# Attention from the seventh tile on in pairs of tiles, 52 weight tiles converted without a maximum, and a new table of attention's release times

## The chip, the core and the metric

One core of a Trainium2 chip runs the whole program. The metric is the device time of one execution in microseconds (us), lower is better. TensorE (PE) does the matmuls, VectorE (DVE), ScalarE (ACT) and GpSimd (POOL) the elementwise work, SyncE (SP) issues the DMAs.

## What is computed

The reference, cut to its core: chunked attention, then two feed-forward layers over all 4608 tokens. The weights come as 64-bit floats.

```python
# q, k, v: (8, 8, 576, 64); chunks of 64 tokens
scores = scale * np.matmul(q_c, k_c.transpose(0, 1, 2, 4, 3))
scores = scores - np.max(scores, axis=-1, keepdims=True)
attn = np.exp(scores)
attn = attn / (np.sum(attn, axis=-1, keepdims=True) + 1e-09)
out = np.matmul(attn, v_c)
...
x = out.transpose(0, 2, 1, 3).reshape(4608, 512)
h = np.maximum(x @ w_in, 0.0)            # w_in (512, 2048)
x = h * h @ w_out                        # w_out (2048, 512)
gate = 1.0 / (1.0 + np.exp(-(x @ w_gate)))   # (512, 1536)
return gate * (x @ w_val) @ w_out2       # (1536, 512)
```

## The kernel before, in words

Attention works on 36 tiles of 128 tokens, all eight heads of a tile together. Six tiles fill two raw buffers of 384 tokens (`raw1`), from which the first feed-forward layer takes its operands. That layer (`plain_unit` for the first six tiles, then `Unit` in the form of Strassen's scheme with seven products) works on these 768 tokens while TensorE does the attention of the next six tiles in between. Every product is a sum over three float32r matmuls per operand pair (high times high, low times high, high times low), so TensorE's work comes in groups of three matmuls with 384 columns (line L689). The operands are made by `split`: ACT writes the high part (L479), DVE the low part (L484). The raw buffers are subtracted from each other on POOL (L493).

For one tile, `attention` has these steps: k and q are turned round on TensorE (L858; from tile 12 on q by DVE from another load), 32 small 64x64 matmuls make the scores in two PSUM banks (L878), DVE takes maximum and difference for each bank (L904, L906), ACT the exponential (L909), DVE the sum (L910) and its inverse (L913, L914), POOL or, from tile 12 on, DVE multiplies (L493), TensorE turns the result round (L924), 32 small matmuls mix it with v (L940), and ACT puts the two banks into `raw1` (L958).

`to_float32` makes a float32 tile from 128x512 words of 64 bits: ACT takes the upper word's absolute value as a float (L526) and scales the lower word (L530), DVE bounds the first from below (L533), shifts it (L537) and puts the sign in (L544), POOL adds the lower word (L551). It is called with `raws`, fixed buffers, for the 16 tiles of the first layer's output weights and the 36 of the second layer (52 tiles), and without for the 16 tiles of the first layer's input weights.

The order on every engine is made by `Plan.run`, a list scheduler over jobs with costs in us. TensorE's jobs are of two kinds. Those of the stream "main", the products, keep their order. Those of the stream "att" are released by a table, `TIMES`: for each tile the due time of the steps k, q, S (scores), T (turning the result) and X (mixing), on an axis whose zero is the first product. At each free moment the ready job with the earliest due time is taken. `Plan.fill` puts matmuls of the identity (L1462) into gaps near the start.

```python
    for j in sorted(cands, key=lambda j: (j.due - self.STAY * (small and j.shared), j.n)):
        if not j.left and take(j):
```

## Time and profile before

| | us |
|---|---|
| median of 3 runs (1600.95 to 1603.32) | 1601.09 |
| profiled execution, its own time | 1601.8 |
| its span, first to last instruction | 1600.0 |
| PE busy in the span | 1584.4 |
| DVE busy | 1306.6 |
| ACT busy | 972.0 |
| POOL busy | 530.8 |

Busy times come from one profiled execution. A matmul's end is modelled, so neighbouring matmuls overlap in the profile; the distance between starts is what a matmul takes in a row of them. What lies outside the span is 1.8 us. A wait of TensorE shows as idle time, or as a start that comes later than the row before it would allow.

### The profile page before, as it was taken

What the parts mean: (1) busy time and instruction counts of PE and PEld (TensorE: products, weight loads), DVE (VectorE), ACT (ScalarE), POOL (GpSimd) and SP (SyncE); (2) the same over time, 40 slices, a digit from 0 to 9 for tenths busy, and PEclk for the clock granted to TensorE, in tenths of its full rate; (3) what the DMA queues carried; (4) which work ended last, traced back from release to release, by engine and by line L of the source; (5) the groups of instructions that cost most, each with busy time, mean ns of one, the idle gap of its engine ahead of it and who ended that gap; (6) DMA issues with size and microseconds to landing.
All of it is one profiled execution on the core that took longest, in us unless ns stands there. A gap on an engine that the chain in (4) does not pass through costs nothing.

```text
span 1600.0 us, 29686 instructions
## 1 busy us (share of the span) xinstructions
PE 1584.4 (99%) x10209; PEld 1387.7 (87%) x10209; DVE 1306.6 (82%) x2170; ACT 972.0 (61%) x1922; POOL 530.8 (33%) x432
## 2 busy tenths in 40 slices
PE   8999999999999999999999999999999999999999
PEld 6998999999998888899888898888888888888888
DVE  6968878797989998999998797743786748889886
ACT  7986676676876656566665665543565545555554
POOL 2452402021442111111266685643576641000000
PEclk9999999999999999999999999999999999999999
DMA  9965667677884848487787547586447577866562
GB/s 214 275 166 143 155 190 187 175 207 218 267 290 148 276 152 261 155 280 241 255 279 267 183 146 244 186 281 217 168 162 245 196 260 257 250 196 164 150 174 52
DMA packets 381991, 333.27 MB, mean 208 GB/s; under 512 B 231824, under 2 KB 292240, under 8 KB 381840
## 3 DMA queue, kind: packets, MB, share of 16 engines
q1 hardware_dynamic: 381840, 331.38, 67.8%
q8 instruction: 80, 1.31, 0.4%
q14 instruction: 71, 0.58, 0.1%
HBM read 209.13 MB, written 122.16 MB: 207 GB/s over the span
## 4 chain that ended last, share of the span: by engine, by line
PE 92%; DVE 3%; ACT 2%; DMA 1%; SPq 1%; issue 1%; POOL 0%; DVEq 0%; ACTq 0%
PE bank L689 51%; PE bank L1097 37%; SPq L457 1%; PE bank L878 1%; PE bank L940 1%; PE bank L924 1%; PE bank L858 1%; DMA wraw__750<-in_moe_w_in_dram 0%; DMA wf<-wf__3185 0%; PE bank L1077 0%; DMA k__326<-in_k_dram 0%; DVE T__2019 L484 0%; DMA gd<-b__3834 0%; DVE B__760 L484 0%; DMA ql__4671<-in_q_dram 0%
## 5 line engine op out<-in xcount | busy, mean ns | idle before, releaser
L551 POOL TENSOR_TENSOR wf__6958<-wf__6958,wr__6912 128x512 int32<-128x512 int32 x18 | 28.2, 1568 | 163.1 <-DVE wf__6958 L544 119.8
L551 POOL TENSOR_TENSOR wf__3185<-wf__3185,wr__3118 128x512 int32<-128x512 int32 x16 | 21.8, 1361 | 174.0 <-DVE wf__3185 L544 120.1
L551 POOL TENSOR_TENSOR wf__7071<-wf__7071,wr__6912 128x512 int32<-128x512 int32 x18 | 25.4, 1413 | 99.0 <-DVE wf__7071 L544 73.2
L493 POOL TENSOR_TENSOR raw__523<-raw__724,raw__523 128x384 f32<-128x384 f32 x20 | 24.2, 1229 | 30.1 <-DVE B__653 L484 12.3
L530 ACT ACTIVATE wr__6912<-wr__6912 128x512 int32<-128x512 uint32 x36 | 23.9, 665 | 0.0
L484 DVE TENSOR_TENSOR wx__7016<-ws__7143,wx__7016 128x512 fp32r<-128x512 f32 x18 | 17.8, 988 | 6.0 <-ACT wx__7016 L479 6.0
L493 POOL TENSOR_TENSOR ws__7143<-wf__7071 128x256 f32<-128x256 f32 x12 | 12.5, 1038 | 30.5 <-DVE wx__7684 L484 29.9
L484 DVE TENSOR_TENSOR wx__7684<-ws__7143,wx__7684 128x512 fp32r<-128x512 f32 x18 | 17.9, 997 | 4.7 <-ACT wx__7684 L479 4.7
L484 DVE TENSOR_TENSOR wx__7154<-wf__7071,wx__7154 128x256 fp32r<-128x256 f32 x18 | 14.2, 787 | 3.5 <-ACT wx__7154 L479 3.5
L479 ACT ACTIVATE wx__7154<-wf__7071 128x256 fp32r<-128x256 f32 x18 | 7.4, 411 | 15.8 <-POOL wf__7071 L551 15.6
L493 POOL TENSOR_TENSOR ws__7143<-ws__7143,wf__6958 128x256 f32<-128x256 f32 x18 | 16.2, 898 | 1.2
L533 DVE TENSOR_SCALAR wf__7071<-wf__7071 128x512 f32<-128x512 f32 x18 | 11.8, 653 | 5.6 <-ACT wf__7071 L526 5.4
L533 DVE TENSOR_SCALAR wf__6958<-wf__6958 128x512 f32<-128x512 f32 x18 | 10.3, 572 | 6.3 <-ACT wf__6958 L526 6.3
L493 POOL TENSOR_TENSOR ws__7143<-wf__6958,wf__7071 128x256 f32<-128x256 f32 x18 | 15.3, 848 | 0.3
L526 ACT ACTIVATE wf__3185<-wr__3118 128x512 f32<-128x512 f32 x16 | 10.6, 664 | 6.9 <-DMA wf<-wf__3185 6.9
L904 DVE TENSOR_REDUCE mx__379<-bank 128x4 f32<-128x256 f32 x16 | 6.6, 415 | 10.0 <-PE bank L878 10.0
L526 ACT ACTIVATE wf__7071<-wr__6912 128x512 f32<-128x512 f32 x18 | 11.9, 662 | 4.4 <-DMA wr__6912<-in_moe_w_gate_dram 1.9
L544 DVE SCALAR_TENSOR_TENSOR wf__6958<-wr__6912,wf__6958 128x512 int32<-128x512 int32 x18 | 14.1, 781 | 0.2
L533 DVE TENSOR_SCALAR wf__3185<-wf__3185 128x512 f32<-128x512 f32 x16 | 8.1, 506 | 7.5 <-ACT wf__3185 L526 7.5
L544 DVE SCALAR_TENSOR_TENSOR wf__7071<-wr__6912,wf__7071 128x512 int32<-128x512 int32 x18 | 13.8, 766 | 0.3
L526 ACT ACTIVATE wf__6958<-wr__6912 128x512 f32<-128x512 f32 x18 | 11.9, 659 | 3.1 <-DVE wod__6685 L484 1.5
L904 DVE TENSOR_REDUCE mx__2010<-bank 128x4 f32<-128x256 f32 x16 | 6.7, 417 | 8.5 <-PE bank L878 8.5
(5753 smaller groups left out, 6044.5 us busy)
## 6 DMA issues: line engine op xcount, KB each, us to landing
ad<-wx__7016 SPq DMA_DIRECT2D x27, 512.0 KB, 4.1
ad<-wx__7684 SPq DMA_DIRECT2D x27, 512.0 KB, 5.1
wr__3118<-in_moe_w_out_dram SPq DMA_DIRECT2D x16, 512.0 KB, 4.6
wr__6912<-in_moe_w_gate_dram SPq DMA_DIRECT2D x12, 512.0 KB, 4.7
wr__6912<-in_moe_w_val_dram SPq DMA_DIRECT2D x12, 512.0 KB, 4.4
wr__6912<-in_moe_w_out_dram SPq DMA_DIRECT2D x12, 512.0 KB, 3.9
ad<-wx__7154 SPq DMA_DIRECT2D x18, 256.0 KB, 3.7
wf<-wf__3185 SPq DMA_DIRECT2D x16, 256.0 KB, 4.5
```

Of the source, the lines that this page charges most:

```text
L457: nc.sync.dma_start(out=a, in_=b)
L484: lambda: nc.vector.tensor_tensor(out=lo(), in0=at(src, n, F32, off), in1=hi().bitcast(F32), op=ALU.subtract),
L493: eng, cost(eng, n), lambda: e.tensor_tensor(out=o(), in0=a(), in1=b(), op=op),
L526: nc.scalar.activation(out=at(w), in_=t[:, :, 1].bitcast(F32), func=ACTF.Abs)
L530: nc.scalar.activation(out=low, in_=low.bitcast(U32), func=ACTF.Copy, scale=2.0**-29)
L533: nc.vector.tensor_scalar_max(at(w), at(w), TINY)
L544: nc.vector.scalar_tensor_tensor(out=wi, in0=words()[:, :, 1], scalar=-0x40000000, in1=wi, op0=ALU.bitwise_and, op1=ALU.bitwise_or,)
L551: nc.gpsimd.tensor_tensor(out=wi, in0=wi, in1=words()[:, :, 0], op=ALU.add)
L689: nc.tensor.matmul(out=o, lhsT=at(op, P, F32R, wi * size + half * HB + kk * P), rhs=at(xb, n, F32R, xi * xsize + off), start=(first and kk ...
L858: nc.tensor.transpose(out=at(ps, P, F32, hp * P), in_=at(r, P, F32, hp * P), identity=ident)
L878: nc.tensor.matmul(out=o[c][to, hp, :], lhsT=qv[part, hp, tok], rhs=kv[part, hp, tok], start=True, stop=True,)
L1097: nc.tensor.matmul(out=at(ps[m], n), lhsT=at(w, P, F32R, wi * size + half * HB + m * P), rhs=at(x, n, F32R, xi * n), start=(first and kp = ...
```

## The change

From tile 6 on, `attention` takes two tiles at a time. The scores of both go into the same two banks (the second tile's into the second half), DVE and ACT work on 512 instead of 256 columns of a bank and on 1024 instead of 512 columns of the rest, one job mixes both tiles, and ACT's copies into `raw1` move both tiles at once where they lie in the same buffer (in every third pair they don't). Turning round stays one job for each tile. `TIMES` has a row for each of the 21 groups and other numbers throughout, also for the first six tiles, which stay single. In `to_float32` the 52 tiles with `raws` lose DVE's maximum; ACT scales by 2^-112 there, and shift counts and sign mask follow.

```diff
+        scale_, left, right, sign = (2.0**-112, 4, 1, -0x80000000) if raws else (1.0, 5, 2, -0x40000000)
...
-            nc.scalar.activation(out=at(w), in_=t[:, :, 1].bitcast(F32), func=ACTF.Abs)
+            nc.scalar.activation(out=at(w), in_=t[:, :, 1].bitcast(F32), func=ACTF.Abs, scale=scale_)
...
-                out=wi, in0=wi, scalar1=5, scalar2=2,
+                out=wi, in0=wi, scalar1=left, scalar2=right,
...
-        job("DVE", 0.41, bound, [w], [w], shared=True)
+        if not raws:
+            job("DVE", 0.41, bound, [w], [w], shared=True)
...
-        (-40, -40, -38, -34, -32),
...
-        (2.5, -1.25, -0.25, -2, 11.5),
...
+        ((-46.25,), (-46.25,), -47.25, (-40.25,), -38.25),
...
+        ((0.5, 4.25), (7.25, -1.5), 2.0, (-2.25, 8.75), 17.5),
...
+    FIRST = 6
+    GROUPS = [(t,) for t in range(FIRST)] + [(t, t + 1) for t in range(FIRST, NTL, 2)]
...
+        def chunk(c):
+            return at(ps_s[c], n * HB).rearrange("p (h k) -> p h k", k=CH)
...
-        job("PE", 0.53, scores, [qT, kT], ps_s, stream="att", at=nominal("S"), shared=True)
+        job("PE", 0.53 * n, scores, list(turned.values()), ps_s, stream="att", at=nominal("S"), shared=True)
...
-            job("DVE", 0.34, lambda c=c: nc.vector.tensor_reduce(
+            job("DVE", (0.34, 0.61)[n - 1], lambda c=c: nc.vector.tensor_reduce(
+                out=largest(c), in_=chunk(c), axis=AX.X, op=ALU.max), [ps_s[c]], [mx])
...
-        job("ACT", 0.53, lambda: nc.scalar.activation(out=at(a), in_=at(a), func=ACTF.Exp, scale=scale), [a], [a])
+        job("ACT", (0.53, 1.0)[n - 1], lambda: nc.scalar.activation(out=at(a), in_=at(a), func=ACTF.Exp, scale=scale),
+            [a], [a])
...
-        mixed = job("PE", 0.66, mix, [aT, vr], ps_x, stream="att", at=nominal("X"), shared=True)
+        mixed = job("PE", 0.66 * n, mix, [*turned_a, *values], ps_x, stream="att", at=nominal("X"), shared=True)
...
+        together = len(set(map(id, to))) == 1
         for c in range(2):
-            job("ACT", 0.27, lambda c=c: put(c), [ps_x[c]], [raw])
+            if together:
+                job("ACT", (0.27, 0.5)[n - 1], lambda c=c: put(c, 0, n), [ps_x[c]], [to[0]])
+                continue
+            for i in range(n):
+                job("ACT", 0.27, lambda c=c, i=i: put(c, i, 1), [ps_x[c]], [to[i]])
```

In the changed kernel the lines are three to twenty-five numbers away: products L692, k and q L855, scores L875, maximum and difference L900 and L902, exponential L905, sum L907, turning L924, mixing L944, puts L965.

How the order moves is seen best behind the first products on TensorE. In the kernel before, the scores of the first two tiles of the second group (each 32 matmuls, in rows of two) stand four product groups apart:

```order
L878 MATMUL bank_75<-kT_32768__876,qT_18432__801 64x64 x2
L878 MATMUL bank_73<-kT_32768__876,qT_18432__801 64x64 x2
L689 MATMUL bank_79<-T_3072_195584__818,wia_83968__799 128x384 x3
L689 MATMUL bank_79<-T_3072_192512__829,wia_83968__799 128x384 x3
L689 MATMUL bank_79<-B_3072_177152__856,wia_83968__799 128x384 x3
L689 MATMUL bank_79<-B_3072_174080__858,wia_83968__799 128x384 x3
L878 MATMUL bank_76<-kT_4608__808,qT_2560__607 64x64 x2
L878 MATMUL bank_77<-kT_4608__808,qT_2560__607 64x64 x2
```

In the changed kernel the same two tiles' scores stand in one block, later among the products, and in the same two banks:

```order
L875 MATMUL bank_75<-kT_28672__870,qT_14336__471 64x64 x2
L875 MATMUL bank_74<-kT_28672__870,qT_14336__471 64x64 x2
L875 MATMUL bank_75<-kT_8192__894,qT_12288__868 64x64 x2
L875 MATMUL bank_74<-kT_8192__894,qT_12288__868 64x64 x2
L875 MATMUL bank_75<-kT_8192__894,qT_12288__868 64x64 x2
L875 MATMUL bank_74<-kT_8192__894,qT_12288__868 64x64 x2
L875 MATMUL bank_75<-kT_8192__894,qT_12288__868 64x64 x2
L875 MATMUL bank_74<-kT_8192__894,qT_12288__868 64x64 x2
L855 MATMUL bank_77<-ident,k_10240__816 128x128 x4
L692 MATMUL bank_78<-B_3072_177152__826,wit_157696__818 128x384 x3
L692 MATMUL bank_78<-B_3072_174080__835,wit_157696__818 128x384 x3
```

What moved: two blocks with products between them became one. Over the whole program, behind the first product, TensorE's order goes from large matmuls to a block of small ones 37 times before and 26 times now, for the same 60 blocks (30 tiles, scores and mixing); behind the first product it has 33 fours of k and q turns before and 35 now, and 30 fours of the result in both.

On DVE, at the same place, before (`a` is the tile of scores, `wia` and `wit` are weight operands, `w` a weight tile in conversion):

```order
L904 TENSOR_REDUCE mx_0__379<-bank_75 128x4
L906 TENSOR_TENSOR a_18432__921<-bank_75,mx_0__379 128x4x64
L904 TENSOR_REDUCE mx_0__379<-bank_73 128x4
L906 TENSOR_TENSOR a_18432__921<-bank_73,mx_0__379 128x4x64
L484 TENSOR_TENSOR wia_79872__883<-w_8704__810,wia_79872__883 128x512
L533 TENSOR_SCALAR w_32768__929<-w_32768__929 128x512
```

and in the changed kernel:

```order
L484 TENSOR_TENSOR wia_79872__876<-w_18432__796,wia_79872__876 128x512
L535 TENSOR_SCALAR w_38912__910<-w_38912__910 128x512
L539 TENSOR_SCALAR w_38912__910<-w_38912__910 128x512
L900 TENSOR_REDUCE mx_5632__959<-bank_75 128x8
L902 TENSOR_TENSOR a_10240__968<-bank_75,mx_5632__959 128x8x64
L900 TENSOR_REDUCE mx_5632__959<-bank_74 128x8
L902 TENSOR_TENSOR a_10240__968<-bank_74,mx_5632__959 128x8x64
L484 TENSOR_TENSOR wit_149504__946<-w_0__846,wit_149504__946 128x512
```

What moved: four operations serve two tiles, each on twice the columns, and they now stand between the second weight group's first operand (`wia`) and its second (`wit`), where before they stood ahead of both. SP's first 18 loads (k, q and v of six tiles) and the first two weight loads behind them are the same in number in both programs.

## Rows read from the trace of the kernel before

**Rows 1.** The page: the span, and each engine's busy time, share and instructions.

```profile
span 1600.0 us, 29686 instructions
...
PE 1584.4 (99%) x10209; PEld 1387.7 (87%) x10209; DVE 1306.6 (82%) x2170; ACT 972.0 (61%) x1922; POOL 530.8 (33%) x432
```

**Rows 2.** The page: the chain that ended last, shares by engine.

```profile
PE 92%; DVE 3%; ACT 2%; DMA 1%; SPq 1%; issue 1%; POOL 0%; DVEq 0%; ACTq 0%
```

**Rows 3.** Three stretches: length, then PE, PEld, DVE, ACT, POOL busy, clock, DMA.

```profile
0.00:35.35 35.35, 28.10 (x509) 22.65 (x510) 22.26 (x53) 24.25 (x50) 9.84 (x14) 1.00 1.05 219
35.35:474.02 438.67, 433.80 (x4240) 413.70 (x4239) 366.97 (x701) 319.18 (x701) 144.94 (x133) 1.00 0.73 205
474.02:1600.00 1125.98, 1122.52 (x5464) 951.33 (x5463) 917.38 (x1418) 628.53 (x1174) 375.99 (x286) 1.00 0.65 209
```

**Rows 4.** TensorE, timeline 43 to 48 us: start, length, line, tiles, count.

```profile
43.72 0.68 PE L689 MATMUL bank<-B__858,wia__799 128*128 128x384 f32 x3
44.33 0.69 PE L878 MATMUL bank<-kT__808,qT__607 64*64 64x64 f32 x32
...
45.59 0.68 PE L689 MATMUL bank<-T__829,wit__820 128*128 128x384 f32 x3
...
47.08 0.68 PE L689 MATMUL bank<-B__858,wit__820 128*128 128x384 f32 x3
47.60 0.68 PE L689 MATMUL bank<-B__653,wia__883 128*128 128x384 f32 x3
```

**Rows 5.** TensorE, timeline 201 to 205 us.

```profile
201.85 0.69 PE L689 MATMUL bank<-B__760,wia__883 128*128 128x384 f32 x3
202.47 0.69 PE L878 MATMUL bank<-kT__2420,qT__2824 64*64 64x64 f32 x32
202.98 0.65 PE L940 MATMUL bank<-aT__2980,v__2726 64*64 64x64 f32 x32
...
204.19 0.68 PE L689 MATMUL bank<-T__2040,wit__820 128*128 128x384 f32 x3
```

**Rows 6.** What TensorE waited for, 35.36 to 474 us: total, times, longest.

```profile
PE bank L689 <- DVE b__2821 L493: 0.9, 1, 0.9
...
PE bank L878 <- ACT h__3040 L464: 0.2, 1, 0.2
```

**Rows 7.** DVE, timeline 141 to 146 us: one tile's own operations.

```profile
141.33 0.42 DVE L904 TENSOR_REDUCE mx__2252<-bank 128x4 f32<-128x256 f32 x1
...
142.64 0.42 DVE L906 TENSOR_TENSOR a__1546<-bank,mx__2252 128x256 f32<-128x256 f32 x1
144.06 0.69 DVE L910 TENSOR_REDUCE mx__2252<-a__1546 128x8 f32<-128x512 f32 x1 [1.00 <-ACT a__1546 L909]
144.78 0.17 DVE L913 TENSOR_SCALAR mx__2252<-mx__2252 128x8 f32<-128x8 f32 x1
144.99 0.20 DVE L914 RECIPROCAL mx__2252<-mx__2252 128x8 f32<-128x8 f32 x1
145.22 0.69 DVE L493 TENSOR_TENSOR a__1546<-a__1546,mx__2252 128x512 f32<-128x512 f32 x1
```

**Rows 8.** Line L533: count, duration in ns (least, median, most), first and last start.

```profile
L533 DVE TENSOR_SCALAR wf__3185<-wf__3185 x16: 386/421/1234, 211.1 to 453.4; 128x512 f32<-128x512 f32 x16
```

**Rows 9.** DVE, timeline at 56 us.

```profile
56.27 1.27 DVE L533 TENSOR_SCALAR w__1028<-w__1028 128x512 f32<-128x512 f32 x1
```

**Rows 10.** POOL, timeline at 56 us.

```profile
55.96 1.30 POOL L493 TENSOR_TENSOR a__921<-a__921,mx__379 128x512 f32<-128x512 f32 x1 [0.44 <-DVE mx__379 L914]
```

**Rows 11.** SP, timeline at 22 us: the first weight load's issue.

```profile
22.20 0.80 SPq L457 DMA_DIRECT2D wraw__588<-in_moe_w_in_dram  x1
```

**Rows 12.** ACT, timeline 28 to 30 us.

```profile
28.46 0.69 ACT L526 ACTIVATE w__735<-wraw__588 128x512 f32<-128x512 f32 x1
29.01 0.69 ACT L530 ACTIVATE wraw__588<-wraw__588 128x512 int32<-128x512 uint32 x1
```

**Rows 13.** TensorE, timeline at 35 us: the first product's first matmul.

```profile
35.35 0.42 PE L689 MATMUL bank<-B__653,wia__799 128*128 128x384 f32 x1
```

224 lines of the change are left out of this document (102 added, 122 removed), and 19 rows, old and new, of the table TIMES.

## The prediction

> **What bounds the kernel now.** I read the page first: TensorE is busy for 1584.4 of 1600.0 us and no other engine over 82% [rows 1], and TensorE has 92% of the chain that ended last [rows 2]. So only what makes TensorE's own work shorter, or takes away its waits, can move the time. Then the stretches [rows 3]. From 474.02 us on, when the first layer is done, TensorE is busy for 1122.52 of 1125.98 us, and its work there is the same in both programs, in the same order: nothing is to be had there. Ahead of 35.35 us lies the start, and between the two lie 438.67 us in which products and attention share TensorE. This middle stretch is where the change acts. DVE is busy for 366.97 us of it, 84%, ACT 73%, POOL 33%.
>
> The busy share hides waits, since the ends of matmuls are modelled. So I made the middle stretch up out of starts. A group of three product matmuls takes 47.60 - 47.08 = 0.52 us [rows 4], and the program has 2064 such matmuls in the first layer: 688 x 0.52 = 357.8 us. Four turns between products take 47.08 - 45.59 - 2 x 0.52 = 0.45 us [rows 4]; 33 fours of k and q and 30 of the result stand behind the first product, 28.4 us. A block of 32 small matmuls alone between products takes 45.59 - 43.72 - 2 x 0.52 = 0.83 us [rows 4]. Two blocks in a row take 204.19 - 201.85 - 2 x 0.52 = 1.30 us [rows 5], so a second block behind a first adds 0.47 and the passage to small matmuls and back costs 0.83 - 0.47 = 0.36 us. With 37 passages and 60 blocks that is 37 x 0.83 + 23 x 0.47 = 41.5 us. The sum is 427.7 us, and 438.67 - 427.7 = 11.0 us are waits. The view of waits names only 4.3 us of them, in ten places, 2.7 us of it ended by DVE, from a DVE add that frees a bank (0.9 us) down to an ACT copy (0.2 us) [rows 6]. I take the same share, 63%, for all: some 7 of the 11 us wait for DVE.
>
> **The change part by part.** *Fewer passages.* TensorE goes to small matmuls 26 times instead of 37 behind the first product, with 60 blocks in both: 11 x 0.36 = 4.0 us less. A block of one kind behind a block of another is what rows 5 show; two score blocks into the same banks have no row. Were a second block to cost as much as a lone one, the gain would be nothing; I take 0.47, since the 32 matmuls inside a block go to the same two banks already.
>
> *Turns moved.* 35 fours of k and q instead of 33 stand behind the first product, so two moved there from the start: 2 x 0.45 = 0.9 us more. In the start TensorE fills time with matmuls of the identity, so there they gave nothing back.
>
> *The start itself.* The first product needs a weight tile that was issued at 22.20 us, behind 18 loads, [rows 11] and that ACT took up at 28.46 us [rows 12], 6.9 us ahead of the first product at 35.35 us [rows 13]. The order of SP has the same 18 loads of the same sizes ahead of that weight tile, in another order, and the second weight tile directly behind it in both. So I take 0. The nearest row for what one step of DMA order is worth is the issue itself, 0.80 us [rows 11]: bounds of -0.8 and +0.8.
>
> *DVE's work.* One tile costs DVE four operations of 0.42 on a bank (maximum and difference, two each), 0.69, 0.17, 0.20, and from tile 12 on 0.69 [rows 7]: 3.43 us, 6.86 for two tiles. A pair's operations on 512 columns of a bank have no row. The difference of 0.69 for 512 and 0.42 for 256 columns [rows 7] is 0.27 us for 256 columns; I take 0.69 for them, and 0.69 + 2 x 0.27 = 1.23 for those on 1024. A pair then costs 4 x 0.69 + 1.23 + 0.17 + 0.20 + 1.23 = 5.59, 1.27 less, over 15 pairs 19 us. If time went with the columns alone, only the two short operations would be saved, 15 x 0.37 = 5.6 us; that is the lower bound, and 15 x 3.43 = 51 the upper, if columns cost nothing. I take 19, because a quarter more columns than the rows cover is a short step along the same line. The maximum falls away 16 times in this stretch, 0.42 us each [rows 8]: 6.7 us. Together DVE does some 26 us less, 341 instead of 367, 78% of the stretch instead of 84%.
>
> *What that does to waits.* DVE's idle share goes from 16% to 22%. A queue's waits go about as busy over idle share, 5.1 before and 3.6 after, so 7 us of waits for DVE become about 5: 2 us less. Bounds: no change, if each wait hangs on the place in the order alone, and 7 us less, if all of it goes. The order is new everywhere, so this term is the least sure.
>
> *What costs and gives nothing.* The other 36 maxima come behind 474 us, where TensorE waits for nobody; DVE's idle time is not the limit there. If that cover were gone, 36 x 0.42 = 15 us would be at stake, but 1122.52 of 1125.98 us busy leaves at most 3.5 us in which anything could be saved. ACT's operation with a scale costs the same as without (0.69 and 0.69, the second with one) [rows 12]. ACT's exponential and puts on double size save some fixed time on an engine that is 27% idle; whoever waits for them waits as before. A pair's multiplication on POOL is one instead of two, three times.
>
> The sum: -4.0 + 0.9 - 2.0 = -5.1 us. The profiled execution took 1601.8 us, 0.7 over the median, so it becomes 1596.7 us, and the median 1601.1 - 5.1 = 1596.0 us.
>
> **The rivals.** *Waits stay as they are.* Then only 4.0 - 0.9 = 3.1 us remain and the time is 1598.0; with a few new waits up to 1601. For it speaks that a wait is made by one late operand at one place, and the new order has such places too; against it that DVE has less to do throughout.
>
> *Most waits go.* The new release times touch every attention step. If 7 of the 11 us go, the time is 1601.1 - 3.1 - 7 = 1591. For it speaks that the waits stand in ten or more single places, each of which a shift of one step can remove; against it that the products' own operands at the change of the 768 tokens are made late in both programs.
>
> *DVE's blocks in the way.* This one is slower. At each pair, four operations of 0.69, 2.8 us, stand together on DVE ahead of what the next product needs, where a tile's took 142.64 + 0.42 - 141.33 = 1.73 us [rows 7]. The order shows it first at the second weight group, where the operand `wit` stands behind such a block. Between the pair's scores and that operand's first product TensorE has one four of turns (0.45 us) and six groups (3.1 us), 3.6 us; DVE needs 2.8 + 0.69 = 3.5 us, and 4.3 us if one collision like that of rows 9 and 10 falls in. So there it is a matter of tenths. If each of the 15 pairs made TensorE wait for 0.6 us more than forecast, that would be 9 us and the time 1605. It decides from 0.55 us for each pair on: 15 x 0.55 = 8.3 us, which is what lies between 1596.0 and 1604.3.
>
> *POOL's longer multiplication.* A DVE operation of usually 0.42 us [rows 8] took 1.27 us, from 56.27 to 57.54 [rows 9], while POOL multiplied from 55.96 to 57.26 [rows 10]: it ended 0.28 us behind POOL. In three pairs, tiles 6 to 11, POOL's operation is twice as wide, 2.6 us by that row, and DVE could stand for 1.3 us longer. If all of it reached TensorE, 3 x 1.3 = 3.9 us, the time would be 1599.9. Against it speaks that the total of POOL's time doesn't grow, so that two short holds become one long. The Trainium skill, SBUF — State Buffer, section "Who interferes with whom", says that whichever of the two issues first gets the shared ports for the whole instruction and the other fully blocks; by that rule, with which rows 9 and 10 agree, the hold is as long as the operation.
>
> **How the numbers follow.** A measurement of this kernel tells about 0.2%, 3.2 us, from no change: faster is below 1597.9, slower above 1604.3. I give the forecast, 1594 to 1598, a chance of 0.42; most waits gone, 1588 to 1594, 0.16; waits as before or a little more, 1598 to 1601.5, 0.23; POOL's hold, 1598 to 1601, 0.06; DVE's blocks, 1601 to 1608, 0.13, of which two thirds lie above 1604.3. So faster has 0.42 + 0.16 = 0.58, and a little of the third case, 0.59; slower 0.09; the rest, 0.32, is no change. The range from 1591 to 1602.5 leaves out about half of the second case and most of the last. For the forecast alone it is 1594 to 1598.
>
> **What would show it.** In the changed kernel's trace, the first product should start at 35.35 us within 0.8; blocks of two tiles' scores should take 1.30 us between products, as in rows 5; a maximum on 512 columns of a bank 0.69 us; DVE's busy time from the first product to the end of the first layer should be about 26 us less; that stretch should be about 5 us shorter than 438.67, and from there on to the end 1126.0 us as before. The same accounting should leave about 9 us of waits. The prediction is wrong if the stretch shrinks by less than 3 or more than 9 us, if the start moves by more than a us, if the part behind 474 us moves at all, or if a second score block in the same banks costs more than 0.47 us.

## The result, and the profile after

The changed kernel takes 1611.59 us (median of six runs, 1609.28 to 1613.64), 1.0062 times the kernel before, 95% interval 1.0052 to 1.0072. That is slower by some 10 us, outside the range that was given. The profiled execution has a span of 1608.9 us, 8.9 over [rows 1].

The page of the changed kernel, span and busy times of the engines:

```profile
span 1608.9 us, 29471 instructions
...
PE 1582.9 (98%) x10207; PEld 1390.1 (86%) x10207; DVE 1272.5 (79%) x2001; ACT 970.1 (60%) x1887; POOL 539.3 (34%) x429
```

TensorE is busy for 1.5 us less than in [rows 1] and DVE for 34 us less, and yet the span is longer: the time went into TensorE's waits. The stretches of the changed kernel, with the columns of [rows 3]; the last two rows are a close look, used further down (the column behind POOL is the granted clock):

```profile
0.00:33.84 33.84, 26.83 (x500) 21.36 (x500) 21.06 (x51) 22.21 (x45) 8.31 (x13) 1.00 1.07 215
33.84:479.27 445.43, 433.19 (x4244) 417.39 (x4245) 351.77 (x570) 317.88 (x670) 150.27 (x130) 0.99 0.72 203
479.27:1608.90 1129.63, 1122.90 (x5465) 951.36 (x5464) 899.64 (x1382) 630.06 (x1174) 380.68 (x286) 1.00 0.65 208
...
128.00:132.44 4.44, 2.56 (x18) 2.26 (x18) 4.34 (x8) 1.89 (x5) 0.00 (x0) 1.00 0.13 30
132.44:135.85 3.41, 3.39 (x11) 2.88 (x10) 3.41 (x9) 1.03 (x4) 0.00 (x0) 0.50 0.36 82
```

Against [rows 3] the start is 1.5 us shorter, the middle 6.8 us longer and the part behind it 3.6 us longer. The accounting of the prediction, applied to the middle: 357.8 us for the products, 65 fours of turns at 0.45, 60 blocks at 0.47 and 26 passages at 0.36 make 424.6 us, 3.1 less than before, as forecast. What is left as waits is 445.4 - 424.6 = 20.8 us in place of 11.0. The view of waits of the changed kernel names the places, first in the middle, then behind it (what TensorE waited for: total, times, longest):

```profile
PE bank L924 <- DVE a__2038 L493: 3.6, 2, 1.9
PE bank L692 <- DVE b__5394 L493: 1.7, 1, 1.7
PE bank L692 <- DVE b__2832 L493: 1.5, 1, 1.5
PE bank L924 <- issue: 1.1, 1, 1.1
...
PE bank L692 <- DVE wit__946 L484: 0.7, 1, 0.7
...
PE bank L1111 <- DVE x__9005 L484: 3.4, 1, 3.4
```

Three kinds stand there: turns of a pair's result (L924) that come before DVE's multiplication is done; products (L692) that come before a DVE add has freed their bank; and one wait of 3.4 us in the second layer (L1111), where the kernel before shows no wait above 0.2 us. In the middle the whole view names 5.8 us in front of turns of the result, where that of the kernel before names none, and some 6 us in front of products, where that of the kernel before names 3.5. The 20.8 us hold one thing more than waits: matmuls that ran at a lower clock, in the row of 132.44 us above and once more (last section).

TensorE's timeline of the changed kernel, start, length, line, tiles, count, and the idle time ahead with what ended it:

```profile
33.84 0.45 PE L692 MATMUL bank<-B__660,wia__787 128*128 128x384 f32 x1 [0.29 <-ACT wia__787 L479]
34.79 0.62 PE L692 MATMUL bank<-B__660,wia__787 128*128 128x384 f32 x2 [0.51 <-DVE wia__787 L484]
...
64.92 0.68 PE L692 MATMUL bank<-B__835,wia__1034 128*128 128x384 f32 x3
65.54 0.69 PE L875 MATMUL bank<-kT__894,qT__884 64*64 64x64 f32 x32
66.06 0.65 PE L875 MATMUL bank<-kT__332,qT__1190 64*64 64x64 f32 x32
...
67.27 0.68 PE L692 MATMUL bank<-T__809,wit__1099 128*128 128x384 f32 x3
...
131.29 1.06 PE L924 MATMUL bank<-ident,a__2038 128*128 128x128 f32 x8 [1.88 <-DVE a__2038 L493]
...
259.51 0.69 PE L692 MATMUL bank<-T__1974,wis__2538 128*128 128x384 f32 x3
...
261.85 0.68 PE L692 MATMUL bank<-B__670,wia__1768 128*128 128x384 f32 x3
```

Two blocks of scores take 67.27 - 64.92 - 2 x 0.52 = 1.31 us between products, and two blocks of mixing 261.85 - 259.51 - 2 x 0.52 = 1.30, as in [rows 5]. So the part of the change that acts on TensorE's own work did what it should.

DVE's timeline of the changed kernel ahead of the turns at 131.29 us, and ahead of the late wait:

```profile
121.41 1.36 DVE L484 TENSOR_TENSOR T__1967<-raw__510,T__1967 128x384 fp32r<-128x384 f32 x1
122.69 1.35 DVE L484 TENSOR_TENSOR T__1974<-raw__510,T__1974 128x384 fp32r<-128x384 f32 x1
123.97 0.68 DVE L900 TENSOR_REDUCE mx__2026<-bank 128x8 f32<-128x512 f32 x1
...
126.17 0.69 DVE L902 TENSOR_TENSOR a__2038<-bank,mx__2026 128x512 f32<-128x512 f32 x1
...
128.18 1.21 DVE L907 TENSOR_REDUCE mx__2026<-a__2038 128x16 f32<-128x1024 f32 x1
...
129.92 1.23 DVE L493 TENSOR_TENSOR a__2038<-a__2038,mx__2026 128x1024 f32<-128x1024 f32 x1
131.06 0.55 DVE L484 TENSOR_TENSOR B__835<-raw__697,B__835 128x384 fp32r<-128x384 f32 x1
...
771.12 0.69 DVE L493 TENSOR_TENSOR g__6810<-g__6475,g__6810 128x512 f32<-128x512 f32 x1
772.16 1.37 DVE L484 TENSOR_TENSOR x__8992<-g__8486,x__8992 128x512 fp32r<-128x512 f32 x1 [0.35 <-ACT x__8992 L479]
777.45 0.69 DVE L493 TENSOR_TENSOR g__6515<-g__6356,g__6515 128x512 f32<-128x512 f32 x1 [3.92 <-DMA g__6356<-gd]
...
778.66 0.68 DVE L484 TENSOR_TENSOR x__9005<-g__8078,x__9005 128x512 fp32r<-128x512 f32 x1
```

From the first maximum at 123.97 to the end of the multiplication at 131.15 us a pair's chain takes 7.2 us, and DVE pauses for no more than 0.2 us in it. Two splits of 384 columns ahead of it take 1.36 and 1.35 us where the split behind it takes 0.55; POOL subtracts beside them without a pause. There are more of such long splits than before: over the middle DVE's splits take 110.13 us in place of 101.18, with nearly the same number. Of them 35 before and 48 now take over 0.15 us more than the usual time of their width, and each of these runs for more than half of its time beside a POOL operation. Stretch, length and busy time of their line (L484 in both), before and now:

```profile
35.35:474.02 438.67, 101.18 (x145) 1.00 0.73 205
```

```profile
33.84:479.27 445.43, 110.13 (x146) 0.99 0.72 203
```

### The profile page after: what moved, and what is told of

Its sections match the earlier page's. It is cut to its first block, busy times and chain, and to the rows that moved or that the text cites. A ratio compares the mean times of both kernels' runs of the same rounds, so it can differ in the third digit from the quotient of the medians.

```text
span 1608.9 us, 29471 instructions
## 1 busy us (share of the span) xinstructions
PE 1582.9 (98%) x10207; PEld 1390.1 (86%) x10207; DVE 1272.5 (79%) x2001; ACT 970.1 (60%) x1887; POOL 539.3 (34%) x429
## 3 DMA queue, kind: packets, MB, share of 16 engines
q8 instruction: 80, 1.31, 0.4%
## 4 chain that ended last, share of the span: by engine, by line
PE 88%; DVE 4%; ACT 2%; issue 1%; DMA 1%; SPq 0%; DVEq 0%; ACTq 0%
PE bank L692 48%; PE bank L1111 37%; PE bank L944 1%; PE bank L875 1%; PE bank L924 1%; PE bank L855 1%; SPq L457 0%; DVE B__695 L484 0%; PE bank L1091 0%; DMA g__6356<-gd 0%; DVE B__689 L484 0%; DMA w__6213<-wf 0%; DMA gd<-c__2049 0%; DVE T__1974 L484 0%; DVE a__2038 L493 0%
## 5 line engine op out<-in xcount | busy, mean ns | idle before, releaser
L553 POOL TENSOR_TENSOR wf__6808<-wf__6808,wr__6764 128x512 int32<-128x512 int32 x18 | 35.6, 1981 | 151.8 <-DVE wf__6808 L546 109.4
L553 POOL TENSOR_TENSOR wf__3199<-wf__3199,wr__3074 128x512 int32<-128x512 int32 x16 | 21.3, 1330 | 165.5 <-DVE wf__3199 L546 51.1
L553 POOL TENSOR_TENSOR wf__6900<-wf__6900,wr__6764 128x512 int32<-128x512 int32 x18 | 26.8, 1486 | 100.1 <-DVE wf__6900 L546 78.1
L493 POOL TENSOR_TENSOR ws__6975<-wf__6900 128x256 f32<-128x256 f32 x12 | 11.3, 942 | 30.7 <-DVE wx__7523 L484 30.0
L484 DVE TENSOR_TENSOR wx__6845<-ws__6975,wx__6845 128x512 fp32r<-128x512 f32 x18 | 16.8, 933 | 3.4 <-issue 1.8
L484 DVE TENSOR_TENSOR wx__7523<-ws__6975,wx__7523 128x512 fp32r<-128x512 f32 x18 | 15.5, 861 | 2.6 <-ACT wx__7523 L479 2.6
L539 DVE TENSOR_SCALAR wf__6808<-wf__6808 128x512 int32<-128x512 int32 x18 | 11.8, 656 | 7.2 <-ACT wf__6808 L528 7.0
L464 ACT ACTIVATE c__2049<-c__2049 128x384 f32<-128x384 f32 x18 | 9.4, 522 | 11.6 <-DVE c__2049 L493 11.4
L546 DVE SCALAR_TENSOR_TENSOR wf__6808<-wr__6764,wf__6808 128x512 int32<-128x512 int32 x18 | 15.8, 879 | 0.3
L546 DVE SCALAR_TENSOR_TENSOR wf__6900<-wr__6764,wf__6900 128x512 int32<-128x512 int32 x18 | 15.8, 879 | 0.3
L539 DVE TENSOR_SCALAR wf__6900<-wf__6900 128x512 int32<-128x512 int32 x18 | 10.9, 603 | 6.1 <-ACT wf__6900 L528 6.1
L484 DVE TENSOR_TENSOR wx__6984<-wf__6900,wx__6984 128x256 fp32r<-128x256 f32 x18 | 13.2, 732 | 2.1 <-ACT wx__6984 L479 2.1
L464 ACT ACTIVATE c__9856<-bank 128x512 f32<-128x512 f32 x6 | 3.6, 598 | 16.7 <-PE bank L692 16.7
L493 DVE TENSOR_TENSOR e__9542<-e__9542,bank 128x512 f32<-128x512 f32 x6 | 4.1, 688 | 10.9 <-PE bank L692 10.8
```

The source lines that it names most:

```text
L484: lambda: nc.vector.tensor_tensor(out=lo(), in0=at(src, n, F32, off), in1=hi().bitcast(F32), op=ALU.subtract),
L493: eng, cost(eng, n), lambda: e.tensor_tensor(out=o(), in0=a(), in1=b(), op=op),
L539: nc.vector.tensor_scalar(out=wi, in0=wi, scalar1=left, scalar2=right, op0=ALU.logical_shift_left, op1=ALU.logical_shift_right,)
L546: nc.vector.scalar_tensor_tensor(out=wi, in0=words()[:, :, 1], scalar=sign, in1=wi, op0=ALU.bitwise_and, op1=ALU.bitwise_or,)
L553: nc.gpsimd.tensor_tensor(out=wi, in0=wi, in1=words()[:, :, 0], op=ALU.add)
```

## The experiments

Eighteen kernels were run. The table has the median, the ratio to the kernel before with its interval, and from the profile in us: the start of the first product, the length of the middle (to the first matmul of 512 columns, 438.5 in the kernel before), the part behind it (1126.2 before), the passages to small matmuls and what the accounting leaves as waits (10.9 before).

| run | median | ratio (95%) | first | middle | behind | passages | waits left |
|---|---|---|---|---|---|---|---|
| changed kernel | 1611.59 | 1.0062 (1.0052-1.0072) | 33.84 | 445.4 | 1129.6 | 26 | 20.8 |
| e1 before, no maximum, planned anew | 1604.85 | 1.0030 (1.0019-1.0040) | 34.55 | 441.4 | 1127.0 | 44 | 11.3 |
| e2 changed, maximum kept, planned anew | 1628.04 | 1.0173 (1.0156-1.0190) | 33.67 | 460.4 | 1132.1 | 28 | 35.1 |
| e3 single tiles, new times | 1639.38 | 1.0241 (1.0223-1.0258) | 34.18 | 474.9 | 1128.6 | 46 | 43.1 |
| e4 pairs, old times | 1704.18 | 1.0648 (1.0632-1.0664) | 34.04 | 539.6 | 1127.1 | 30 | 114.0 |
| f1 order of changed, maximum back | 1619.18 | 1.0108 (1.0093-1.0124) | 33.16 | 449.1 | 1137.0 | 26 | 24.6 |
| f2 order of before, no maximum | 1599.60 | 0.9989 (0.9980-0.9998) | 35.95 | 435.7 | 1126.2 | 37 | 8.1 |
| f3 order of changed, wide operations halved | 1613.12 | 1.0072 (1.0059-1.0085) | 33.84 | 445.1 | 1129.6 | 26 | 20.6 |
| f4 changed, one load moved | 1605.80 | 1.0029 (1.0020-1.0039) | 33.91 | 443.7 | 1127.2 | 26 | 19.1 |
| f5 f4, stretch written out anew | 1633.13 | 1.0201 (1.0188-1.0215) | 33.96 | 443.7 | 1153.1 | 27 | 18.7 |
| f6 f2, stretch written out anew | 1628.23 | 1.0169 (1.0155-1.0183) | 35.72 | 446.5 | 1146.6 | 40 | 17.8 |
| f7 f4, few jobs moved | 1607.68 | 1.0042 (1.0029-1.0054) | 34.16 | 445.4 | 1130.3 | 27 | 20.4 |
| f8 f2, few jobs moved | 1599.98 | 0.9994 (0.9985-1.0003) | 35.97 | 435.8 | 1126.2 | 37 | 8.2 |
| g1 f4, no multiplication on DVE | 1602.72 | 1.0005 (0.9996-1.0015) | 34.38 | 439.0 | 1127.0 | 26 | 14.4 |
| g2 f4, no subtractions on POOL | 1601.08 | 0.9998 (0.9989-1.0007) | 33.80 | 437.0 | 1126.9 | 26 | 12.4 |
| n1 before, turns 0.25 us earlier | 1622.15 | 1.0130 (1.0113-1.0147) | 34.60 | 458.9 | 1127.0 | 44 | 28.8 |
| n2 changed, turns 0.25 us earlier | 1639.96 | 1.0239 (1.0223-1.0254) | 33.69 | 472.4 | 1131.0 | 28 | 47.1 |
| n3 before, scores and turns 0.25 us earlier | 1613.13 | 1.0075 (1.0058-1.0092) | 35.44 | 446.6 | 1126.5 | 44 | 16.5 |
| n4 changed, scores and turns 0.25 us earlier | 1648.28 | 1.0293 (1.0278-1.0308) | 33.91 | 483.5 | 1127.8 | 28 | 58.2 |

**Parts of the change by themselves, planned anew (e1 to e4).** The edits: only the conversion's part of the diff on the kernel before; the maximum kept in the changed kernel; and the two crossings of grouping and table:

```diff
# e1 (on before) and, reversed, e2 (on the changed kernel)
-        job("DVE", 0.41, bound, [w], [w], shared=True)
+        if not raws:
+            job("DVE", 0.41, bound, [w], [w], shared=True)
# e3: a tile takes the times of its pair
-    GROUPS = [(t,) for t in range(FIRST)] + [(t, t + 1) for t in range(FIRST, NTL, 2)]
+    GROUPS = [(t,) for t in range(NTL)]
# e4: a pair takes the old times of its tiles (the mean for S and X)
-        row = dict(zip("kqSTX", TIMES[GROUPS.index(tiles)]))
+        rows_ = [dict(zip("kqSTX", OLD[t])) for t in tiles]
```

> The kernel before, with only the maximum taken out of the 52 conversions; its planner makes a new order from the old release times. In that order TensorE passes to small matmuls 44 times behind the first product instead of 37, which at 0.36 us each is 2.5 us more. Theory M (taking the maximum out moves the conversions, and the late wait of 3.4 us at 775 us comes from that): 1601.5 + 2.5 + 3.4 = 1607, with a wait of 3 us or more between 700 and 800 us. Theories P (the pairs' longer steps) and R (the new release times): no late wait, about 1604, with no wait of over 1.2 us for a turn of the result.

> The changed kernel with the maximum back in all 52 conversions, pairs and the new release times kept; 28 passages. Theory M: the late wait goes, about 1608, and the waits for turns of the result stay. Theories P and R: the waits for turns stay (5 us or more in all), and they say nothing on the late wait: 1608 to 1613.

> The changed kernel with single tiles throughout, each with its own part of the new release times (scores and mixing at the pair's time); 46 passages, 9 more than before, 3.2 us. Theory P: the waits for the turn of the result go, and the middle stretch is that of the kernel before plus the passages: about 1604 without a late wait, 1607 with one. Theory R: the turns still come too early for what DVE has done, with the passages 1611 or more.

> The changed kernel, pairs and no maximum, with the release times of the kernel before (each tile's own for k, q and the turn of the result, the mean of the two for scores and mixing); 30 passages, 7 fewer than before, 2.5 us. Theory R: the waits for turns go, about 1599, or 1602.5 with a late wait. Theory P: waits for turns as in the changed kernel or more, 1608 or more.

e1 came out near the 1604 of theories P and R, but not all of what they said holds: a turn of the result waits 2.0 us, where 1.2 was the most, and that with single tiles. e2 is far above what any theory gave. e3 and e4 lie in the open ends of R (1611 or more) and P (1608 or more), so far up that neither explains them. All were planned anew, and with the job set the order changed everywhere: e1 has 44 passages in place of 37, 2.5 us by the prediction's price, which is most of its loss. e4 has one wait of 72.6 us for a q turned by DVE. So such runs mix a part of the change with a new order. In all that follow but n1 to n4 nothing is planned anew: the planned order is kept, or single jobs in it are moved.

**The maximum at a fixed order (f1, f2).** The planned job stays where it was; only its instruction is left out or put back:

```diff
# f2, on before (with the new constants of the conversion)
-            nc.vector.tensor_scalar_max(at(w), at(w), TINY)
+            if not raws:
+                nc.vector.tensor_scalar_max(at(w), at(w), TINY)
# f1, on the changed kernel (with the old constants)
         def three():
+            if raws:
+                bound()
```

> The changed kernel's order of instructions kept as it is on every engine, and the maximum put back into the 52 conversions (one more DVE operation in front of the first shift, with the old constants). Theory O (the order decides, DVE's work hardly): DVE gets 52 operations more, 16 of them in the middle stretch, 6.7 us there; TensorE's waits stand at the same places and grow by 0 to 2 us in all, time 1611 to 1614. Theory D (DVE's load makes the waits, as the prediction's queue rule has it): waits grow in proportion, 2 to 4 us, time 1614 to 1616. If the 3.4 us wait at 779 us comes from POOL being kept off while DVE's operations follow without a gap, it stays or grows, as one operation more stands in front of POOL's addition.

> The kernel before with its own order kept on every engine, and only the 52 maxima left out (conversion with the new constants). Theory O: the removal by itself is worth 0 to 1 us, time 1600 to 1601, and the 44 passages and 3 us more of the replanned version without the maximum (1604.85) came from the replanned order. Theory D: DVE's idle share in the middle stretch rises from 16 to 18 percent, waits shrink by 1 us or more, time 1599 to 1600. Theory S (without the maximum, POOL's additions start in the middle of a dense row of DVE operations and are kept off): POOL operations of 5 us and more appear behind 474 us, and TensorE waits there, time 1603 to 1605.

f2 gained 0.1% by its interval, with the order of before: 2.8 us of the middle. Theory D put it at 1599 to 1600, and the median is there; the interval alone, 1598.5 to 1601.4, reaches into the range of O too. Of theory S nothing came: the part behind the middle is as before. f1 lost more than any theory said: 3.7 us in the middle, and 7.4 behind it, where the late wait grew from 3.4 to 5.7 us and TensorE's granted clock was 0.50 for 6.83 us from 783.97 on, during that wait and behind it. In the order of the changed kernel the removal of the maximum is a gain of some 7 us. At a fixed order the conversion is therefore no loss in either kernel. Planned anew, the same instructions cost more both times: e1 has 5 us over f2 and e2 9 us over f1.

**The wide operations (f3).**

```diff
-            job("DVE", (0.34, 0.61)[n - 1], lambda c=c: nc.vector.tensor_reduce(
-                out=largest(c), in_=chunk(c), axis=AX.X, op=ALU.max), [ps_s[c]], [mx])
+            job("DVE", (0.34, 0.61)[n - 1], lambda c=c: [nc.vector.tensor_reduce(
+                out=largest(c)[:, x], in_=chunk(c)[:, x], axis=AX.X, op=ALU.max) for x in each(HP)], [ps_s[c]], [mx])
...
```

> The changed kernel's order kept on every engine; each of the pair's wide DVE operations (maximum, difference, sum, and from tile 12 on the multiplication) is issued as two of half the size, as a single tile has them. By the prediction's price that is 1.27 us more of DVE for each pair, 19 us over 15 pairs. Theory O (late chains at a few places): each chain from the scores to the turns gets 0.9 to 1.3 us longer, which shows in full at the five places where TensorE waits for the turns and at some others, 6 to 12 us, time 1617 to 1624. Theory D (queue rule): 19 us more of DVE take back what was forecast, about 1.5 us, time 1613. Theory W (the wide operations stand in the way of what the products need): no more than 1 us is added, or some is gained, time 1610 to 1612.

The time cannot be told from that of the changed kernel (1613.12 and 1611.59, the intervals overlap). Theory D named 1613, but for 19 us more of DVE, and DVE's busy time in the middle is 355.35 us against 351.77, 3.6 us more. By the durations some 13 were to be expected of these operations (0.90 for each of 15 pairs, less the multiplications that POOL does; the 19 count the short operations too, which f3 does not halve). DVE's timeline of f3 shows why:

```profile
274.54 0.75 DVE L903 TENSOR_REDUCE mx__3868<-bank 128x4 f32<-128x256 f32 x2
```

Two maxima in a row take 0.75 us, not 2 x 0.42: the second starts 0.08 us before the first has ended. Against 0.68 for the wide one the saving is 0.07 us. But halves in a row are not what single tiles have. There a maximum and its difference take turns, and two tiles' operations on the banks take 2 x 1.73 = 3.46 us [rows 7]; the pair's four take 126.86 - 123.97 = 2.89 us, timeline above. That is 0.57 us less, near the 0.60 of the prediction. So f3 prices the halves, and not what the wide operations saved.

**The late wait (f4).** In the changed kernel POOL's addition and SP's queue read like this (POOL's timeline, then SP's):

```profile
765.42 7.56 POOL L553 TENSOR_TENSOR wf__6808<-wf__6808,wr__6764 128x512 int32<-128x512 int32 x1 [22.21 <-DMA g__6475<-gd]
```

```profile
761.89 0.37 SPq L457 DMA_DIRECT2D g__8952<-gd  x1
773.00 0.38 SPq L457 DMA_DIRECT2D wr__6764<-in_moe_w_val_dram  x1
773.49 0.45 SPq L457 DMA_DIRECT2D g__6356<-gd  x1
```

The addition took 7.56 us, the next load into the buffer that it reads stood at the head of SP's queue until it was done, and the load of `g__6356` behind it came too late for DVE (3.92 us idle, above), and so for TensorE.

```diff
+        loads = [j for j in plan.order if j.eng == "SP" and any(b.name == "wr" for b in j.bufs)]
+        wr = loads[27]
+        plan.behind([(wr, plan.nth("SP", wr, 8))])
```

`behind` and `nth` are new helpers: the load goes behind the eighth job that follows it in SP's queue, and all other instructions keep their order.

> The changed kernel with one change of order: the load of a weight tile of the second layer that stood in SP's queue from 762 to 773 us, waiting for POOL's addition of 7.56 us, is issued behind the eight loads of g instead of in front of them. Theory Q (the queue passes the delay on): the g loads issue some 9 us earlier, DVE does not wait for g, the wait of 3.4 us at 779 us goes, the late part falls from 1129.6 to 1126.2, time 1608.2. Rival: the next product operand is late on DVE for another reason, the wait stays, time 1611.6. POOL's addition takes 7.5 us in either case.

The wait is gone, though POOL's addition still takes 7.56 us, and the part behind the middle is 2.4 us shorter: theory Q is shown. Theory Q had 1608.2 and the median is 1605.80: the middle is 1.7 us shorter too, though nearly every single wait is still there; what differs is TensorE's clock, below. e1 has an addition of the same 7.56 us, and no late wait.

**Moving jobs (f5 to f8).** The order of the jobs in the middle was written out by number, for the pairs and, as a control, for single tiles without the maximum:

```diff
+        again = [plan.jobs[int(n)] for n in AGAIN.split()]
+        i = plan.order.index(min(again, key=plan.order.index))
...
+        plan.order[i:i + len(again)] = again
         plan.emit()
```

> The changed kernel with the same jobs, tiles in pairs and no maximum, with the load of the weight tile moved as in the run before, and the order of its jobs from about 62 us to the end of the first layer written out anew: single jobs on DVE, ACT, POOL, SP and TensorE stand some places earlier or later, with more room between a pair's scores and its turns and between the second last product of a unit and the add that frees its bank. Passages of TensorE to small matmuls stay nearly as many (26 to 27 behind the first product). Theory O (the waits come from where this table of release times puts the steps): the waits left of 19 us fall to 5 to 12, the middle stretch from 443.7 to 430 to 437, time 1592 to 1599, below the kernel before. Rival P (pairs by themselves make TensorE wait, since a pair's chain from scores to turns takes some 7.5 us and its wide operations stand in blocks on DVE): waits stay at 15 us and more, time 1602 or more.

> The control: single tiles as before, the 52 maxima left out, and the order of the jobs in the same stretch written out anew in the same way as for the pairs. The run with the order of before took 1599.6 with 8 us of waits left. Theory O: waits fall to 4 to 8 us, time 1596 to 1600; the difference to the respaced pairs is what the pairs are worth, 3 to 5 us by passages and start. Rival P: this one falls by 2 us or more and the respaced pairs stay behind it.

> The changed kernel with the load of the weight tile moved (that run: 1605.8, middle stretch 443.7 us, 19 us of waits left) and, between 62 us and the end of the first layer, some hundred jobs moved a few places: 12 on TensorE, 28 on DVE, 50 on ACT, 8 in SP's queue, none on POOL; durations and landings stay those of the trace, and nothing that the second layer needs is put off. In the run before (all jobs of the stretch written out anew) the moves also put off the second layer's loads, and the waits were only exchanged. Theory O (single late operands at single places make the waits): waits left fall from 19 to 8 to 12 us, the middle stretch to 433 to 437, time 1595 to 1600. Rival P (pairs make TensorE wait wherever they stand): waits go from one place to the next, 16 us and more stay, time 1603 or more.

> The control for it: single tiles in the order of before without the 52 maxima (that run: 1599.6, middle stretch 435.7 us, 8 us of waits left), with moves made in the same way: 5 jobs on TensorE, 26 on DVE, 26 on ACT, 5 in SP's queue. Theory O: waits left fall from 8 to 3 to 6 us, time 1595 to 1598, some 2 us behind or level with the pairs. Rival P: this one gains 2 to 4 us, and the pairs stay 5 us or more behind it.

None of them gained. f5 and f6 put off what the second layer needs (waits of 5.7 and 8.4 us at 524 and 549 us in f5), so their total says nothing, and their middles are no shorter. f7 removed the waits for the bank adds at 339 and 412 us nearly or wholly and got others: 1.7 us for an ACT copy at 131, 2.1 at the turns at 211. Its waits left are 20.4 us against 19.1 in f4, with a stretch of lower clock in the middle of the profiled execution (1611.66 us, 4 over the median). Behind the middle POOL's addition took 15.71 us there, and TensorE waited 2.2 us in spite of the moved load. By the medians f7 (1607.68) cannot be told from f4 (1605.80). That is what rival P said, pairs that make TensorE wait wherever they stand; but f8 gained nothing either, against both theories, so moves of this kind may only be a bad tool.

**What the waits hang on (g1, g2).** On f4, the order kept. g1 leaves out the multiplication by the inverse sums in 12 pairs, so the attention result stays undivided; g2 leaves out POOL's subtractions of tokens in the first layer, so products get wrong operands:

```diff
# g1, at the multiplication
+        skip = eng == "DVE"
+        (binary if not skip else lambda e, o, x, y, op, n, ob, ib: job(
...
# g2, in the subtraction of tokens
+                if n != BL1:
+                    binary("POOL", part(oo), part(xx), part(yy), ALU.subtract, n, [oo[0]], {oo[0], xx[0], yy[0]})
+                    continue
+                job("POOL", cost("POOL", n), lambda: None, {oo[0], xx[0], yy[0]}, [oo[0]], shared=True)
```

> The changed kernel with the load of the weight tile moved (1605.8; 19 us of waits left in the middle stretch, 6.4 us of them at the turns), order kept, and the multiplication by the inverse sums left out in the 12 pairs where DVE does it, 1.22 us each: the attention result stays undivided, so the output is not the reference's. Chain: each chain from scores to turns is 1.2 us shorter, the turns' waits of 2.05, 1.27, 1.36, 0.88 and 0.59 us shrink to 1.2 or less together, what stands behind on DVE comes earlier too, the middle stretch falls by 5 to 8 us, time 1598 to 1601. Hold: the turns' waits shrink, but the adds in front of the bank products stay late, 3 to 4 us, time 1602 to 1603. Table (waits hang on places that are not DVE's): 2 us or less, time 1604 or more.

> The changed kernel with the load of the weight tile moved, order kept, and POOL's subtractions of the tokens in the first layer left out (the splits read what stands in their input, so the output is not the reference's). DVE's splits of 384 columns beside them take 1.35 us in place of 0.55. Hold: without them the splits at 121, 338 and 412 us take 0.55 us, the waits of 2.05 us at 132, 1.64 at 339 and 1.88 at 412 fall by 1.5 each, the middle stretch by 5 to 8 us, time 1598 to 1601. Chain: only the bank products at 339 and 412 gain, 2 to 4 us, time 1602 to 1604. Table: 2 us or less, time 1604 or more.

The first rows of TensorE's waits in the middle, of g1 and then of g2 (there L927 is the line of the turns):

```profile
PE bank L692 <- issue: 1.9, 1, 1.9
PE bank L692 <- DVE b__5382 L493: 1.6, 1, 1.6
PE bank L692 <- DVE b__2028 L493: 1.5, 1, 1.5
```

```profile
PE bank L927 <- DVE a__2031 L493: 3.7, 2, 2.1
PE bank L927 <- issue: 1.1, 1, 1.1
PE bank L927 <- DVE a__1257 L493: 0.7, 1, 0.7
```

In g1 no turn waits any more, and the adds stay late (8.6 us of named waits of products, 6.7 in f4); in g2 the turns wait as before (5.5 us of named waits, 5.3 in f4), and the named waits of products fall from 6.7 us in f4 to 1.6. The middle is 4.7 us shorter in g1 and 6.7 in g2. How the subtractions reach TensorE is seen in f4 ahead of its wait at 339 us (TensorE, DVE and POOL; L750, L542 and L551 are the lines of products, splits and adds there):

```profile
338.72 0.79 PE L750 MATMUL bank<-T__2052,wid__2697 128*128 128x384 f32 x3 [1.47 <-DVE b__2832 L551]
...
335.56 1.37 DVE L542 TENSOR_TENSOR B__689<-raw__510,B__689 128x384 fp32r<-128x384 f32 x1
336.85 1.35 DVE L542 TENSOR_TENSOR B__695<-raw__510,B__695 128x384 fp32r<-128x384 f32 x1
338.12 0.54 DVE L551 TENSOR_TENSOR b__2832<-b__2832,bank 128x384 f32<-128x384 f32 x1
...
335.25 2.53 POOL L551 TENSOR_TENSOR raw__510<-raw__697,raw__510 128x384 f32<-128x384 f32 x2 [6.85 <-DVE B__660 L542]
```

So both causes are there, side by side: the length of DVE's chain makes the turns late, and POOL's subtractions, which stretch DVE's splits, make the adds late. The kernel before has such chains and subtractions too; what it would gain by the same two omissions was not run. At 131 us Hold was wrong: in g2 the splits there take 0.55 us and the turns come 1.9 us earlier than in f4, at 130.04, but so does all that TensorE has ahead of them, and the wait stays at 2.1 us.

**A quarter of a microsecond (n1 to n4).** The release times of T, or of S and T, from tile 6 on, 0.25 us earlier, planned anew (here n1; n3 has "ST", n2 and n4 the same in the changed kernel):

```diff
+    TIMES = [[x + -0.25 if x is not None and t >= 6 and nm in "T" else x for nm, x in zip("kqSTX", row)]
+             for t, row in enumerate(TIMES)]
```

> The kernel before with the release times of the turns of the result 0.25 us earlier from tile 6 on, planned anew. Table: the order changes in many places and the time with it, by 5 us or more to the slow side, 1606 to 1620. Chain or Hold: a quarter of a us changes little, 1600 to 1604.

> The changed kernel with the release times of the turns of the result 0.25 us earlier from tile 6 on, planned anew. Table: a new draw, anywhere from 1600 to 1630, 5 us or more away from 1611.6. Chain or Hold: 1610 to 1615, with waits at the turns as before.

> The kernel before with the release times of scores and turns 0.25 us earlier from tile 6 on, planned anew. Table: again 5 us or more to the slow side, 1606 to 1630. If the first shift was a fluke: 1600 to 1604.

> The changed kernel with the release times of scores and turns 0.25 us earlier from tile 6 on, planned anew. Table: 1615 to 1645. If pairs by themselves were no worse than single tiles, this lies as far above 1611.6 as the run beside it above 1601; a much larger distance speaks for pairs being harder to place.

n1 and n3 are 21 and 12 us over the kernel before, n2 and n4 28 and 37 us over the changed one. Theory Table has the direction right for both kernels, and each shift is worth more than the 5 us that it asked for, which Chain or Hold do not explain; but n1, n2 and n4 came out 2, 10 and 3 us above the ranges that Table gave. A quarter of a us in the table is worth more than the whole change. The idle time in front of the turns of the result comes to 12.8 and 16.5 us in n2 and n4, 7.5 and 7.3 of it in one place each, and to 2.1 and 3.4 in n1 and n3; with shifted tables, pairs did worse than single tiles both times. Only two shifts, both to the early side, were run, so that is no law, and whether other tables would suit either kernel better is open.

## Why the prediction was wrong, point by point

**Fewer passages, turns moved: right.** 26 passages, 60 blocks and 65 fours, 3.1 us less by the accounting, and a second block of one kind costs 1.30 - 0.83 = 0.47 us, as was taken.

**The start: a term missed, small size.** Forecast 0 within 0.8, measured -1.5 at the first product, of which its second matmul gave back 0.3 (34.79 us; 35.98 before). I looked at loads alone. In the kernel before, turns of q stood right ahead of the first product and waited for their load. But its second matmul, behind which the rest follows, waited for DVE's split of `wia`, and that split ran beside an addition of POOL's (TensorE, DVE and POOL, the kernel before):

```profile
34.94 0.66 PE L858 MATMUL bank<-ident,q__739 128*128 128x128 f32 x4 [0.35 <-DMA q__739<-in_q_dram]
...
35.98 0.62 PE L689 MATMUL bank<-B__653,wia__799 128*128 128x384 f32 x2 [0.21 <-DVE wia__799 L484]
...
34.13 1.79 DVE L484 TENSOR_TENSOR wia__799<-w__735,wia__799 128x512 fp32r<-128x512 f32 x1
...
33.88 1.49 POOL L551 TENSOR_TENSOR w__741<-w__741,wraw__627 128x512 int32<-128x512 int32 x1 [1.15 <-DMA q__739<-in_q_dram]
```

In the changed kernel the split starts at the same time, ahead of that addition, and takes 0.68 us; the split behind it takes the hold (DVE and POOL):

```profile
34.05 0.68 DVE L484 TENSOR_TENSOR wia__787<-w__713,wia__787 128x512 fp32r<-128x512 f32 x1
34.66 1.67 DVE L484 TENSOR_TENSOR B__695<-raw__510,B__695 128x384 fp32r<-128x384 f32 x1
...
34.36 1.55 POOL L553 TENSOR_TENSOR w__746<-w__746,wraw__638 128x512 int32<-128x512 int32 x1 [1.23 <-ACT raw__697 L965]
```

That accounts for the 1.2 us that lasted: it is the collision of [rows 9] and [rows 10], which the new order moved to another split.

**DVE's work: right in direction, mis-sized.** Forecast 26 us less in the middle, measured 366.97 - 351.77 = 15.2. The maxima are worth 366.97 - 358.60 = 8.4 us (f2), a little over the 6.7 of the forecast. By the busy times of their lines, a tile's maxima, differences and sums fell from 70.61 to 59.37 us, the two short operations from 13.88 to 6.69, about what was forecast or more. Such sums count twice the 0.08 us for which operations in a row overlap, and so did mine. What the sum left out is the splits: nearly as many as before, they take 9.0 us more, because more of them fall beside POOL. I had used that collision ([rows 9], [rows 10]) for POOL's multiplication alone.

**What that does to waits: this step failed, and it decides.** I turned a busy share into waits, 2.0 us less, and set the worst bound at no change. The accounting has 11 us before and 20.8 after, 9.9 us more, a part of which is the lower clock. The share of DVE did fall, from 84 to 79%, and at a fixed order less work on DVE gave fewer waits, more than such a rule gives (f2: 2.8 us less for 8.4 us of DVE, where the rule has some 0.9). But the changed kernel has another order, and its waits hang on single late operands: turns on the end of DVE's chain (g1), products on adds behind long splits (g2). The rival of waits that stay had this argument; I gave it at most a few new waits, up to 1601.

**DVE's blocks in the way: half right.** This rival was put at 1605, with a chance of 0.13. The place that it named is there, 0.7 us for `wit__946`. But a pair's four operations on the banks are a small part; most of the new time goes to the turns behind the pair's sum and multiplication and to bank adds behind stretched splits. POOL's longer multiplication, the fourth rival, shows nowhere as a wait of TensorE; at 52.69 us it took 1.91 us, not the 2.6 of the estimate.

**Nothing to be had behind the middle: wrong.** I looked only for what could be saved there, and not for what could be lost: the part grew by 3.5 us, with one wait of 3.4 us behind a load held up in SP's queue. The moved load of f4 gives 2.4 of the 3.5 us back in the profile; in the medians, with the clock's part, it is 5.8.

**Still open:** how much of the new waits is due to the pairs and how much to the order that this table gives them, and whether another table would make pairs faster than single tiles. Without their waits they have 3 us less to do. No version of the pairs with the whole computation beat the kernel before; the only run that did, by 0.1%, is f2, single tiles in the old order with the maxima taken out.

## What to carry to other kernels

A gain in work on the bounding engine is safe only as far as the order around it stays; where a scheduler makes the order from hand-set times, a new order is a new draw, and its waits have to be read from its own trace. To size one part of a change, freeze the order and take out the instruction alone: planned anew, the same part read as a loss of 0.3%, frozen as a gain of 0.1%. Price an operation in a row by the distance from start to start, not by its duration, and only in the order in which it will stand. Look at which operations run beside another engine that holds them up, and look at each queue for a transfer that stands behind one late instruction.

## What the chip showed that I had not expected

A POOL operation can be kept off far longer than one DVE operation. The addition at 765.42 us took 7.56 us, usually 1.3, while DVE ran operations of 0.69 us with no pause, all with both inputs in SBUF; it ended 1.17 us after the begin of DVE's first pause, 771.81 to 772.16 us, and the DVE operation behind that pause took 1.37 us. In f7, where DVE ran on without a pause to 780.8 us, it took 15.71. All runs together have 19 POOL operations of over 3.3 us: 14 ended 1.15 to 1.17 us after the begin of DVE's first pause, and two more (e3 at 637.48 us, n1 at 583.63) 1.2 to 1.3 us after the start of a DVE operation that reads a PSUM bank. In the middle DVE is held up instead: its splits of 0.55 us took 1.36 and 1.35. The Trainium skill, SBUF — State Buffer, section "Who interferes with whom", says that issue order decides who blocks. As I read that rule, POOL, whose row starts at 765.42, should have gone ahead of the DVE operation that started at 765.70; the trace shows ten later DVE operations done before it, so here the measurement goes against the rule. Each of the ten started some 0.09 us before the one ahead had ended; whether that kept POOL off was not tried.

TensorE's clock fell in the changed kernel to a granted 0.50, 1.2 in place of 2.4 GHz, for 3.41 us behind the wait of 1.88 us that ended at 131.29 us, and again for 3.41 us from 210.94, behind the wait of 1.68 us that ended at 209.46. The kernel before ran at 1.00 through the whole middle [rows 3]. Behind the waits of 1.46 and 1.73 us at 341 and 414 us it did not fall, nor behind the 3.41 us at 779. f4 has 1.00 all through the middle with nearly the same waits (1.89 us at 131.91), and is 1.7 us shorter there. Compared matmul by matmul, the changed kernel falls behind f4 by some 0.7 us across the first stretch and by 1.4 across the second; f4 loses a part again in waits of its own. In n4, with 58 us left by the accounting, such stretches add up to 34 us of the middle. So a wait of TensorE can cost more than it lasts, by an amount that differs from run to run.
